# Moving a one-column constant so that the streamed matmul operands start 32 bytes earlier in SBUF

## The chip, the cores and the metric

One Trainium2 chip, one of its cores. The metric is the device time of one execution in microseconds (us). TensorE is PE in the profile (its weight loads are the row PEld), VectorE is DVE, ScalarE is ACT, GpSimd is POOL and SyncE is SP.

## The reference

A gated linear attention (4 batches, 8 heads, 768 steps, head size 48, a complex decay per channel) feeds a feed-forward block with a leaky ReLU. Cut to what matters here:

```python
for t in range(S):                      # per batch and head
    S_re, S_im = a_re_n * S_re - a_im_n * S_im + k v^T, a_re_n * S_im + a_im_n * S_re
    y[t] = q[t] @ S_re
x = y.reshape(3072, 384)                # tokens by channels
h = x @ w_in                            # 384 -> 2048
out = np.maximum(0.01 * h, h) @ w_out   # 2048 -> 384
```

## The kernel before, in words

The tokens are cut into 24 units of 128 (one chunk of one batch each). Attention is done in chunked form: `prep` (line 655) makes running decay products on DVE and ACT, `relay_of` (line 860) moves them to another partition layout by DMA, and `attend` (line 904) makes scores, masks them and forms the 128 output columns of its unit. Two units make one group `g` of `GT` = 256 tokens; there are 12 groups.

The feed-forward part works on one group at a time and splits every fp32 operand into a high part of type fp32r and a remainder, also fp32r. `attend` leaves the group's input as the tile `x` (high and low part, each 3 blocks of 256 columns). `first(g, s)` (line 1062) makes a block of `h`: for each of 2 blocks of 128 hidden channels and each of the 3 blocks of `x` it does three matmuls, high by high, high by low, low by high. `hide` (line 1074) applies the leaky ReLU on ACT and DVE and splits the result into the tile `hid`. `second(g, s)` (line 1089) streams `hid` against `wout_hi` and `wout_lo` into three banks of PSUM. So a group has 8 x 18 matmuls of `first` and 8 x 18 of `second`, 288 in all, and the kernel has 12 x 288 = 3,456 of them. In each, the weights (128 x 128 of `win_hi`, `win_lo`, `wout_hi` or `wout_lo`) are stationary and are loaded for that matmul, and 256 columns of `x` or `hid` are streamed: 1,024 contiguous bytes in each partition.

The four weight tiles are made at the start by `convert` (line 582) from 64-bit data. Its PE part (lines 641 to 643) has three matmuls per slab of 384 columns: two in fp32 against `ident`, and one in fp32r that streams a slab of `win_hi` or `wout_hi` against the stationary `nid`.

The order on each engine is set at build time: `drive` (line 236) runs all tasks against planned costs, and `Lane` (line 102) chains each engine's instructions in the planned order. The planner's costs are functions of shapes and kinds of instructions; they do not look at addresses. All compute instructions go through one call in `Lane`, so nearly all rows of the profile carry its line, 111.

Where things lie in a partition follows from the order of the pools and the sizes of the tiles; each tile begins at a multiple of 32 bytes. The pool `keep` comes first (`acc`, `xacc`, `low`, `zfl`, `wacc`, `bad`: 96, 96, 32, 288, 96 and 32 bytes), then the pool `cp`:

```python
win_hi, win_lo, wout_hi, wout_lo   # 24,576 bytes each
ident, mask, pst, rst              # 512, 2,048, 96 and 7,168 bytes
lnc                                # 4 bytes, so 32 of its own
nid                                # 512 bytes
```

and then the pool `pp` with everything that is worked on: two buffers of `asb` (2,048 bytes each), `qkt` (12,384), `t96` (16,512), two of `x` (6,144), `v` (6,656), two of `a` (9,216), `kn` and the output staging (3,072 each), a staging tile (6,144), three of `hid` (4,096), then `sq`, `u1`, `qk`, `xs`, `tg` and small ones. From `x` to `hid` all these sizes are multiples of 512 bytes.

`lnc` holds the logarithm of 0.999. It is written once by DVE (line 498) and read by ACT as the bias of one `Exp` per attention stage (line 689). `low` holds four sums that ACT writes in the last stage (lines 853 and 855) and that DVE reads in the final check (line 279).

Of the kernel before, what the change touches and what calls it, by code (L numbers as in the profile page):

```python
# [7 lines left out]
F32 = mybir.dt.float32  # L8
# [13 lines left out]
P = 128  # L22
# [406 lines left out]
def body(ctx, tc, keep, a_in, qk_in, v_in, w_in, out):  # L429
    nc = tc.nc  # L430

    cp = ctx.enter_context(tc.tile_pool(name="cp", bufs=1))
# [13 lines left out]
    nsub = len(SUBS)  # L446
    acc = keep.tile([P, 2, nsub], F32, tag="acc", name="acc")
    xacc = keep.tile([P, NT // C], F32, tag="xacc", name="xacc")
    low = keep.tile([P, 4], F32, tag="low", name="low")
    zfl = keep.tile([P, nsub, 2 * TI], F32, tag="zfl", name="zfl")  # L450
    lnc = cp.tile([P, 1], F32, tag="lnc", name="lnc")
    wacc = keep.tile([P, 2, WCP * -(-NWC // WCK)], F32, tag="wacc", name="wacc")

    pe, dve, act = Lane(tc, nc.tensor, pe_cost), Lane(tc, nc.vector, dve_cost), Lane(tc, nc.scalar, act_cost)
# [813 lines left out]
```

## Time and profile before

| | |
|---|---|
| median of 3 runs | 635.88 us (634.34 to 636.84) |
| the profiled execution | 636.34 us |
| its span, first to last instruction | 634.6 us |
| mean granted TensorE clock | 0.979 |
| PE busy | 593.1 us, 93% of the span |
| DVE busy | 531.2 us, 84% |
| ACT busy | 378.6 us, 60% |

The busy time of an engine is the union of its instructions' times, so a PE that is busy all the time need not be at its peak: the matmuls are pipelined, and a row's mean duration is the latency of one matmul, which is longer than the distance from one start to the next (called the pitch below). The pitch is read from the starts in a timeline, or from a piece of the chain of waits that counts its instructions. [...]

### The profile page before, as it was taken

To read this page: it belongs to the slowest core of one execution; us is meant where nothing else is said; L and a number is where in the kernel's file an instruction comes from. 1 tells how busy PE (TensorE), PEld (TensorE's weight loads), DVE (VectorE), ACT (ScalarE), POOL (GpSimd) and SP (SyncE) were. 2 spreads that over 40 slices of the span, in tenths; PEclk is the share of its full clock that TensorE was granted. 3 is DMA by queue.
4 is the path that set the end of the run, shared out by engine and by line. 5 is a ranking of instruction groups with operands and counts; after the bars stand their busy time and mean duration, and the time that the engine had idled before them with its cause. 6 is when DMAs were issued, how large, how long until landed. Compare 5 with 4: busy or idle time off the path is not lost.

```text
span 634.6 us, 18137 instructions
## 1 busy us (share of the span) xinstructions
PE 593.1 (93%) x7714; PEld 554.4 (87%) x7714; DVE 531.2 (84%) x916; ACT 378.6 (60%) x838; POOL 10.2 (2%) x33
## 2 busy tenths in 40 slices
PE   4992999999989989999999999999999999999994
PEld 2451668899889979999999999999999999999994
DVE  6999999899898988999989989999999898644340
ACT  6975776465475474574764664664755734868641
POOL 2000100100000000000000000000000000000000
PEclk9996999999999989999999999999999999999998
DMA  8843721422424223233235044043142235667500
GB/s 347 323 133 121 250 80 52 152 80 60 142 82 119 83 76 102 106 98 106 81 108 173 3 131 150 14 150 120 56 125 104 89 108 186 185 207 269 194 1 30
DMA packets 30200, 79.25 MB, mean 125 GB/s; under 512 B 5120, under 2 KB 11264, under 8 KB 30112
## 3 DMA queue, kind: packets, MB, share of 16 engines
q1 hardware_dynamic: 29728, 77.23, 37.5%
q8 instruction: 62, 1.02, 0.6%
q0 software_dynamic: 384, 0.79, 0.5%
q14 instruction: 26, 0.21, 0.1%
HBM read 54.26 MB, written 4.72 MB: 93 GB/s over the span
## 4 chain that ended last, share of the span: by engine, by line
PE 64%; DVE 23%; DMA 5%; ACT 4%; issue 2%; SPq 0%; DVEq 0%; ACTq 0%
PE ph L111 26%; PE po L111 26%; PE att L111 11%; DMA a<-in_a_dram 4%; DVE qkt L111 4%; DVE a L111 4%; DVE u L111 3%; DVE hid L111 2%; PE pd L111 2%; DVE sq L111 2%; DVE tg L111 1%; DVE xs L111 1%; DVE asb L111 1%; ACT sq L111 1%; DVE wcv L111 1%
## 5 line engine op out<-in xcount | busy, mean ns | idle before, releaser
L111 PE MATMUL po<-hid,wout_hi 128*128 128x256 f32 x1152 | 224.8, 284 | 0.0
L111 PE MATMUL ph<-x,win_hi 128*128 128x256 f32 x1152 | 217.3, 287 | 5.5 <-ACT x L111 3.3
L111 PEld LDWEIGHTS ph<-x,win_hi 128*128 128x128 f32 x1152 | 180.7, 191 | 7.9 <-ACT x L111 3.5
L111 PEld LDWEIGHTS po<-hid,wout_hi 128*128 128x128 f32 x1152 | 184.3, 189 | 1.2 <-issue 0.6
L111 PE MATMUL ph<-x,win_lo 128*128 128x256 f32 x576 | 164.1, 285 | 0.0
L111 PE MATMUL po<-hid,wout_lo 128*128 128x256 f32 x576 | 143.2, 284 | 0.0
L111 PEld LDWEIGHTS ph<-x,win_lo 128*128 128x128 f32 x576 | 109.7, 190 | 0.0
L111 PEld LDWEIGHTS po<-hid,wout_lo 128*128 128x128 f32 x576 | 109.2, 190 | 0.0
L111 ACT ACTIVATE tg<-ph 128x512 f32<-128x512 f32 x96 | 57.0, 594 | 74.2 <-PE ph L111 74.2
L111 DVE TENSOR_TENSOR tg<-ph,tg 128x512 f32<-128x512 f32 x96 | 65.7, 686 | 35.7 <-ACT tg L111 35.5
L111 ACT CAST hid<-tg 128x512 fp32r<-128x512 f32 x96 | 59.1, 616 | 47.5 <-DVE tg L111 47.3
L111 DVE TENSOR_TENSOR hid<-tg,hid 128x512 fp32r<-128x512 f32 x96 | 65.7, 686 | 14.3 <-ACT hid L111 13.4
L111 DVE TENSOR_TENSOR u<-a 128x384 f32<-128x384 f32 x84 | 46.5, 554 | 2.9 <-ACT a L111 1.4
L111 DVE TENSOR_TENSOR qkt<-qk,a 128x768 f32<-128x768 f32 x48 | 45.1, 952 | 3.9 <-ACT qkt L111 3.7
L111 PE MATMUL att<-t 96*32 96x96 f32 (+3 forms) x1536 | 38.0, 251 | 2.5 <-DMA t<-qkt 0.9
L111 PEld LDWEIGHTS att<-t 96*32 96x32 f32 x1536 | 33.7, 144 | 6.7 <-issue 1.5
L111 PE MATMUL att<-asb,v 128*32 128x128 f32 x768 | 37.1, 275 | 0.1
L111 ACT ACTIVATE rst<-rst,t 96x48 f32<-96x48 f32 x128 | 30.6, 322 | 8.3 <-DVE rst L111 8.3
L111 ACT COPY kn<-att 128x384 f32<-128x384 f32 x40 | 18.9, 476 | 27.5 <-PE att L111 23.0
L111 PE MATMUL att<-t,rst 96*32 96x128 f32 x640 | 32.3, 272 | 0.0
L111 DVE TENSOR_TENSOR asb<-att,mask 128x512 f32<-128x512 f32 x48 | 31.0, 683 | 1.1 <-PE att L111 0.9
L111 DVE TENSOR_TENSOR a<-u 128x192 f32<-128x192 f32 x84 | 29.8, 354 | 1.8
(171 smaller groups left out, 777.8 us busy)
## 6 DMA issues: line engine op xcount, KB each, us to landing
t<-qkt SPq DMA_DIRECT2D x92, 145.1 KB, 3.0
wck<-in_w_dram SPq DMA_DIRECT2D x10, 1152.0 KB, 6.1
v<-in_v_dram SPq DMA_DIRECT2D x12, 832.0 KB, 4.4
a<-in_a_dram SPq DMA_DIRECT2D x12, 768.0 KB, 4.7
qk<-in_qk_dram SPq DMA_DIRECT2D x12, 768.0 KB, 5.9
out_dram<-ot SPq DMA_DIRECT2D x12, 384.0 KB, 2.7
t<-qkt SPq DMA_DIRECT2D x46, 64.5 KB, 2.5
stage_st<-in_w_dram SPq DMA_DIRECT2D x3, 768.0 KB, 9.2
```

What stands on the lines that cost most here:

```text
L111: x = getattr(self.engine, name)(*args, **kw)
```

## The change

The tile `lnc` in the pool `cp` goes away. `low`, in the pool `keep`, gets a fifth column, and `lnc` becomes a view of that column.

```diff
-    low = keep.tile([P, 4], F32, tag="low", name="low")
+    low = keep.tile([P, 5], F32, tag="low", name="low")
     zfl = keep.tile([P, nsub, 2 * TI], F32, tag="zfl", name="zfl")
-    lnc = cp.tile([P, 1], F32, tag="lnc", name="lnc")
+    lnc = low[:, 4:5]
```

With 20 bytes instead of 16, `low` still fills one block of 32 bytes. `cp` is 32 bytes shorter, so `nid` and every tile of `pp` begin 32 bytes earlier. `x` and `hid` began at a multiple of 512 bytes plus 96 and now begin at a multiple of 512 plus 64. The four weight tiles, `ident`, `mask`, `pst` and `rst` lie ahead of `lnc` and stay where they were. No instruction is added, removed or reordered by the text of the change.

## Rows read from the trace of the kernel before

**Rows 1.** The page: busy time and instructions of each engine.

```profile
PE 593.1 (93%) x7714; PEld 554.4 (87%) x7714; DVE 531.2 (84%) x916; ACT 378.6 (60%) x838; POOL 10.2 (2%) x33
```

**Rows 2.** The chain that ended last: its shares by line.

```profile
by line: PE ph L111 25.7%; PE po L111 25.6%; PE att L111 11.3%; DMA a<-in_a_dram 4.5%; DVE qkt L111 4.3%; DVE a L111 4.1%; DVE u L111 3.4%; issue 2.2%; DVE hid L111 1.7%; PE pd L111 1.7%; DVE sq L111 1.6%; DVE tg L111 1.4%; DVE xs L111 1.1%
```

**Rows 3.** Busy time by stretch: us, PE, PEld, DVE, ACT, POOL, PEclk, DMA, GB/s.

```profile
20.00:40.00 20.00, 18.34 (x57) 9.98 (x56) 19.79 (x38) 16.50 (x30) 0.16 (x1) 1.00 0.70 255
...
344.69:389.38 44.69, 44.69 (x658) 43.87 (x657) 41.13 (x70) 26.43 (x64) 0.12 (x1) 1.00 0.32 98
389.38:434.07 44.69, 44.69 (x659) 43.89 (x657) 41.13 (x70) 26.42 (x64) 0.12 (x1) 1.00 0.32 103
...
500.00:600.00 100.00, 100.00 (x1229) 97.75 (x1221) 64.44 (x104) 62.45 (x124) 0.12 (x1) 1.00 0.60 193
```

**Rows 4.** Groups by line: the feed-forward matmuls (busy, mean ns of one).

```profile
L111 PE MATMUL po<-hid,wout_hi 128*128 128x256 f32 x1152 | 224.8, 284 | 0.0
L111 PE MATMUL ph<-x,win_hi 128*128 128x256 f32 x1152 | 217.3, 287 | 5.5 <-ACT x L111 3.3 <-DVE x L111 1.3 <-DVE tg L111 0.9
...
L111 PE MATMUL ph<-x,win_lo 128*128 128x256 f32 x576 | 164.1, 285 | 0.0
L111 PE MATMUL po<-hid,wout_lo 128*128 128x256 f32 x576 | 143.2, 284 | 0.0
```

**Rows 5.** The chain in order of time, 326 to 336 us (start, us, what).

```profile
326.99 4.32 PE po L111 x36
331.31 4.32 PE ph L111 x36
```

**Rows 6.** Timeline near 30.6 us: the weight conversion on PE and PEld.

```profile
30.61 0.19 PEld L111 LDWEIGHTS pd<-wout_hi,nid 128*128 128x128 f32 x1 [1.43 <-ACT wout_hi L111]
30.61 0.44 PE L111 MATMUL pd<-wout_hi,nid 128*128 128x384 f32 x1 [0.79 <-ACT wout_hi L111]
30.72 0.36 PEld L111 LDWEIGHTS pd<-stage_v,ident 128*128 128x128 f32 x2
...
30.89 0.50 PE L111 MATMUL pd<-stage_v,ident 128*128 128x384 f32 x1
```

**Rows 7.** Timeline near 607 us: feed-forward matmuls and their weight loads (start, us).

```profile
606.99 0.28 PE L111 MATMUL po<-hid,wout_lo 128*128 128x256 f32 x1
606.99 0.19 PEld L111 LDWEIGHTS po<-hid,wout_hi 128*128 128x128 f32 x1
607.11 0.28 PE L111 MATMUL po<-hid,wout_hi 128*128 128x256 f32 x1
607.11 0.19 PEld L111 LDWEIGHTS po<-hid,wout_lo 128*128 128x128 f32 x1
...
607.23 0.29 PE L111 MATMUL po<-hid,wout_lo 128*128 128x256 f32 x1
607.23 0.19 PEld L111 LDWEIGHTS po<-hid,wout_hi 128*128 128x128 f32 x1
```

**Rows 8.** The tiles lnc and low: durations (min/median/max), first and last start.

```profile
L111 ACT ACTIVATE u<-u,lnc x12: 926/936/941, 9.0 to 492.7; 128x768 f32<-128x768 f32 x12
L111 DVE MEMSET lnc<- x1: 59/59/59, 2.0 to 2.0; 128x1 f32 x1
...
L111 DVE TENSOR_SCALAR scr<-low x4: 142/142/143, 611.5 to 611.7; 128x1 f32<-128x1 f32 x4
```

**Rows 9.** Timeline of PE near 308 us: attention's output matmuls.

```profile
307.80 0.41 PE L111 MATMUL att<-t,rst 96*32 96x128 f32 x8
308.02 0.40 PE L111 MATMUL att<-asb,v 128*32 128x128 f32 x8
308.24 0.40 PE L111 MATMUL att<-t,rst 96*32 96x128 f32 x8
308.46 0.40 PE L111 MATMUL att<-asb,v 128*32 128x128 f32 x8
```

**Rows 10.** Groups by line: DVE instructions of the same shape on different tiles.

```profile
L111 DVE SCALAR_TENSOR_TENSOR qkt<-qkt 128x768 f32<-128x768 f32 x12 | 11.4, 949 | 0.0
L111 DVE TENSOR_TENSOR sq<-sq 128x768 f32<-128x768 f32 x12 | 11.4, 949 | 0.0
```

**Rows 11.** The chain in order of time: the pieces of the first loads.

```profile
0.82 4.50 DMA a<-in_a_dram
...
65.57 6.46 DMA a<-in_a_dram
```

## Prediction

> **What bounds the kernel now.** I read the busy times first: PE is at work for 593.1 of 634.6 us [rows 1]. That alone says little of a pipelined engine, so the chain of waits comes next: the feed-forward matmuls of `first` and `second` hold 25.7% and 25.6% of it, attention's matmuls 11.3%, and DVE's lines lie between [rows 2]. Then the stretches: a group takes 44.69 us in the middle, in which PE never pauses and DVE works for 41.13 us; after 500 us DVE is at 64% and PE still at 100% [rows 3]. So over most of the span the pitch of the matmuls sets the time, with DVE close behind it. Their durations of 284 to 287 ns [rows 4] are latencies. The pitch stands in the chain: 36 matmuls in 4.32 us, twice in a row, for `hid` and for `x` alike, which is 120 ns each [rows 5]. All 3,456 together are 3,456 x 0.120 = 414.7 us, and the chain's 51.3% are 325.6 us, so 79% of them lie on the path that sets the end.
>
> **What 120 ns are made of** decides the case, since x and hid are the operands that the change moves. [...] In the weight conversion a matmul of the same type streams 384 columns of `wout_hi`; its weights and those of the next matmul are issued 0.11 us apart, and the next matmul begins 0.28 us after it [rows 6]. Taking the first load off, the stream lasted 0.28 - 0.11 = 0.17 us. [...]
>
> This is the row that I lean on. The sizes in the text of the kernel put `wout_hi` at a multiple of 512 bytes plus 256: `x` is at plus 96, `asb`, `qkt` and `t96` ahead of it put the start of `pp` at plus 384, and the 108,672 bytes of `cp` ahead of that put its start, and each weight tile, at plus 256. [...]
>
> [...] Each feed-forward matmul begins together with the load of the next weights, and the next such pair comes 0.12 us later [rows 7]; two loads that nothing holds up come 0.11 us apart [rows 6]. A load that may start only when the matmul before it has taken its weights gives a loop of 0.11 us and a handover of some 10 ns, which is 120 ns whatever the stream needs, as long as the stream ends within it. The weight tiles don't move. In the conversion the load (0.11) is shorter than the stream (0.17), so there the stream decides.
>
> **The change, part by part.** Taken away: one tile; the write to `lnc` stays (59 ns, once, at 2.0 us), and the 12 activations that read it stay (936 ns) [rows 8]. Cost: 0. Reading the bias from `low` might add an order between those reads, the last at 492.7 us, and the writes to `low` after it; both are ACT's, in that order already, and DVE reads `low` at 611.5 us only [rows 8]. Cost: 0, and no one waits newly. No queue gets another order, SP's and POOL's included, since the planner's costs don't see addresses.
>
> Moved by 32 bytes: `nid` and all of `pp`. For attention's matmuls `asb` goes from a multiple of 128 (plus 384) to plus 352. The rows hold both kinds side by side: eight with `asb` as the stream and eight with `t96`, whose slices begin at steps of 516 bytes, take 0.22 us each, turn by turn [rows 9]. Cost: 0; with a rounding step of 0.01 us in each turn the bound is 5% of attention's 11.3%, or 3.6 us either way. For DVE the intermediate halves of `qkt` begin 3,096 bytes into their tile, which is no multiple of 16, and take 949 ns like `sq` [rows 10]. Cost: 0. For the loads by DMA no row shows one size at two offsets; the pieces of the chain that hold them are 4.50 us at the start and 6.46 us at 65.57 us [rows 11]. I take 0; a tenth of these two, 1.1 us either way, is the bound.
>
> Moved by 32 bytes too, and the question itself: `x` and `hid`. I take 0, by the loop above. [...]
>
> [...]
>
> The sum is 0. The profiled execution took 636.34 us, 1.7 beyond its span and 0.5 above the median, so I forecast **636.0**, the median. What a measurement of this kernel can tell from no change is about 0.5%, 3.2 us.
>
> **Rivals.**
>
> *A, the stream is the bound and its start costs.* [...] Against: the loop of loads gives 120 without it. [...]
>
> *B, the moved stream meets the weight load.* Both read SBUF in the same 120 ns; the weights stay at plus 256 and the stream shifts against them. Place: each feed-forward matmul. [...] For: nothing between 96 and 64 is measured, so a worse place is as open as a better one. [...]
>
> *C, nothing moves*, because the constant's block had stood elsewhere than the text implies. Then the time stays, as in the forecast, and I count it there.
>
> **How the numbers follow.** No change, the loop of loads or C, gets 0.49: two independent rows speak for it, but both rest on starts rounded to 0.01 us. A gets 0.36, as the kernel spends half its chain in exactly the operands that move, and B 0.15. The likeliest case alone would lie between 632 and 640, by attention's 3.6 us either way with the loads' 1.1 largely inside. The range takes in B's 646 and, on A's side, its 627 and half of the way on to 613, to 618; beyond these I leave out about 0.15. Faster by over 0.5% is A, slower B.
>
> **What would show it.** [...] The group's 44.69 us follows by 288 pitches, and if it shrinks, DVE's share of it must rise above 41.13 of 44.69. Eight attention matmuls should keep 0.22 us, `sq` and `qkt` 949 ns, `lnc`'s activation 936. The forecast is wrong if the pitch differs from 120 ns by more than 1.1 ns (3.2 us on the 79%), whatever the reason; it is wrong in its reason if the pitch stays and the time still moves, for then one of the parts costed at 0 has a price.

## The result, and the profile after

The changed kernel takes **630.43 us** (median of 10 runs, 628.78 to 633.21) against 636.52 for the kernel before (10 runs, 634.34 to 640.63): a ratio of 0.9900, 95% interval 0.9876 to 0.9924. That is 6.1 us or 1.0% faster. The forecast was no change; the time lies inside the range given, but on rival A's side.

The page of the changed kernel, busy time and instructions by engine, which answers to [rows 1]:

```profile
PE 586.4 (93%) x7714; PEld 546.8 (87%) x7714; DVE 530.3 (84%) x916; ACT 378.0 (60%) x838; POOL 10.1 (2%) x33
```

PE has the same number of instructions and 6.7 us less work, its weight loads 7.6; no other row changes by as much as 1 us. The span is 629.3 us, 5.3 less than before. Next the chain of waits of the changed kernel, its shares by line, its first load (against [rows 11]) and the two pieces that answer to [rows 5] (start, us, what):

```profile
by line: PE po L111 26.0%; PE ph L111 24.6%; PE att L111 15.6%; DVE a L111 4.3%; DVE qkt L111 3.9%; DVE u L111 3.1%; DMA a<-in_a_dram 2.6%; issue 2.4%; DVE hid L111 1.8%; DVE sq L111 1.6%; PE pd L111 1.4%; DVE tg L111 1.4%; DVE asb L111 1.3
...
0.82 4.57 DMA a<-in_a_dram
...
326.16 4.24 PE po L111 x36
330.40 4.24 PE ph L111 x36
```

36 matmuls take 4.24 us where they took 4.32: 117.8 ns for each instead of 120. Here is the change, and it is the same for `hid` and for `x`. The table by stretch (us, PE, PEld, DVE, ACT, POOL, PEclk, DMA, GB/s) says the same of a group; its rows answer to those of the middle in [rows 3]:

```profile
326.50:370.55 44.05, 44.05 (x659) 43.24 (x658) 41.04 (x70) 26.57 (x65) 0.12 (x1) 1.00 0.33 102
370.55:414.60 44.05, 44.05 (x658) 43.24 (x657) 41.04 (x70) 26.50 (x65) 0.12 (x1) 1.00 0.33 102
```

44.05 instead of 44.69 us: 0.64 less, and 288 pitches shorter by 2.2 ns are 0.63. The granted clock is 1.00 in these stretches of both kernels, so the clock is not the cause. DVE's 41.04 us stay below the group's time.

What the prediction had costed at nothing stayed where it was, as far as rows show it. First attention's output matmuls of the changed kernel in PE's timeline (against [rows 9]: eight in 0.22 us, turn by turn), then the tile `low`, which now holds the constant (against [rows 8]; duration min/median/max in ns), then the two DVE groups of [rows 10]:

```profile
307.17 0.40 PE L111 MATMUL att<-t,rst 96*32 96x128 f32 x8
307.39 0.40 PE L111 MATMUL att<-asb,v 128*32 128x128 f32 x8
307.61 0.40 PE L111 MATMUL att<-t,rst 96*32 96x128 f32 x8
307.83 0.40 PE L111 MATMUL att<-asb,v 128*32 128x128 f32 x8
```

```profile
L111 ACT ACTIVATE u<-u,low x12: 926/937/940, 9.0 to 489.6; 128x768 f32<-128x768 f32 x12
...
L111 DVE MEMSET low<- x1: 59/59/59, 2.0 to 2.0; 128x1 f32 x1
```

```profile
L111 DVE TENSOR_TENSOR sq<-sq 128x768 f32<-128x768 f32 x12 | 11.4, 950 | 0.0
L111 DVE SCALAR_TENSOR_TENSOR qkt<-qkt 128x768 f32<-128x768 f32 x12 | 11.4, 949 | 0.0
```

In the chain, attention's share rose from 11.3% to 15.6% and that of the loads of `a` fell from 4.5% to 2.6%. The matmuls above are as long as before, and the first load takes 4.57 us where [rows 11] has 4.50; the shares say by which waits the path ran in one execution, not how long a thing takes. No row isolates the price of the moved loads.

**Where in the span the time was saved.** ACT copies each group's result out of PSUM when its last matmul is done; these copies date the groups. From ACT's timeline of the kernel before, groups 0, 3, 4 and 11 (start, us, instruction, idle time before it):

```profile
139.58 0.93 ACT L111 COPY ot<-po 128x256 f32<-128x256 f32 x3
...
286.41 0.92 ACT L111 COPY ot<-po 128x256 f32<-128x256 f32 x3 [1.30 <-PE po L111]
...
331.11 0.92 ACT L111 COPY ot<-po 128x256 f32<-128x256 f32 x3 [1.56 <-PE po L111]
...
626.27 0.92 ACT L111 COPY ot<-po 128x256 f32<-128x256 f32 x3 [4.21 <-PE po L111]
```

The same four of the changed kernel:

```profile
141.66 0.93 ACT L111 COPY ot<-po 128x256 f32<-128x256 f32 x3
...
286.13 0.92 ACT L111 COPY ot<-po 128x256 f32<-128x256 f32 x3 [1.09 <-PE po L111]
...
330.21 0.93 ACT L111 COPY ot<-po 128x256 f32<-128x256 f32 x3 [1.41 <-PE po L111]
...
621.13 0.92 ACT L111 COPY ot<-po 128x256 f32<-128x256 f32 x3 [4.09 <-PE po L111]
```

After the first group the changed kernel is 2.1 us late, at the fourth it is 0.3 us ahead, and at the end 5.1. So of the 5.3 us in the span nearly all come from the eight groups behind 286 us, some 0.6 us each. Ahead of 286 us PE pauses. In the trace of the kernel before, PE is busy for 36.83 of the 50 us from 50 to 100, 44.33 of the 47 from 140 to 187 and 48.69 of the 52 from 187 to 239. DVE works for 47.31, 44.73 and 45.08 us of these, the chain ahead of 286 us holds loads of `a` of 5.34 to 6.75 us, and the granted clock falls to 0.86 in the first and 0.90 in the last. The clock between 50 and 100 us was 0.86 in the profiled execution before and 0.80 in that of the changed kernel, which goes with the late first group; one kernel profiled twice, below, shows a difference of this kind without any change of the layout.

### The profile page after: what moved, and what is told of

It is laid out like the page before. It is cut to its first block, busy times and chain, and to the rows that moved or that the text cites. A ratio compares the mean times of both kernels' runs of the same rounds, so it can differ in the third digit from the quotient of the medians.

```text
span 629.3 us, 18137 instructions
## 1 busy us (share of the span) xinstructions
PE 586.4 (93%) x7714; PEld 546.8 (87%) x7714; DVE 530.3 (84%) x916; ACT 378.0 (60%) x838; POOL 10.1 (2%) x33
## 4 chain that ended last, share of the span: by engine, by line
PE 68%; DVE 22%; ACT 4%; DMA 3%; issue 2%; DVEq 0%; ACTq 0%
PE po L111 26%; PE ph L111 25%; PE att L111 16%; DVE a L111 4%; DVE qkt L111 4%; DVE u L111 3%; DMA a<-in_a_dram 3%; DVE hid L111 2%; DVE sq L111 2%; PE pd L111 1%; DVE tg L111 1%; DVE asb L111 1%; ACT qkt L111 1%; DVE stage_st L111 1%; ACT sq L111 1%
## 5 line engine op out<-in xcount | busy, mean ns | idle before, releaser
L111 PE MATMUL po<-hid,wout_hi 128*128 128x256 f32 x1152 | 220.2, 282 | 0.0
L111 PE MATMUL ph<-x,win_hi 128*128 128x256 f32 x1152 | 210.6, 282 | 3.5 <-DVE x L111 1.2
L111 PEld LDWEIGHTS po<-hid,wout_hi 128*128 128x128 f32 x1152 | 182.0, 188 | 1.2 <-issue 0.6
L111 PEld LDWEIGHTS ph<-x,win_hi 128*128 128x128 f32 x1152 | 175.9, 187 | 6.1 <-DVE x L111 1.6
L111 PE MATMUL ph<-x,win_lo 128*128 128x256 f32 x576 | 160.7, 279 | 0.0
L111 PE MATMUL po<-hid,wout_lo 128*128 128x256 f32 x576 | 140.0, 279 | 0.0
L111 PEld LDWEIGHTS ph<-x,win_lo 128*128 128x128 f32 x576 | 108.2, 188 | 0.0
L111 PE MATMUL att<-t 96*32 96x128 f32 (+3 forms) x1536 | 37.8, 251 | 3.3 <-DMA t<-qkt 2.3
L111 ACT ACTIVATE rst<-rst,t 96x48 f32<-96x48 f32 x128 | 30.6, 323 | 8.7 <-DVE rst L111 8.7
L111 ACT ACTIVATE wck<-wck 128x1152 f32<-128x1152 f32 (+1 forms) x22 | 27.5, 1250 | 6.4 <-DMA wck<-in_w_dram 6.3
```

The lines of the kernel that those rows point to most:

```text
L111: x = getattr(self.engine, name)(*args, **kw)
```

## The experiments

Two things changed at once: the place of the constant and the start of all streamed tiles. And the start itself can matter in two ways: by itself (rival A's mechanism), or by its **distance** to the weights that are loaded while the stream runs (rival B's, with the sign open). In all that follows the distance is the stream's start less the weights' start, modulo 512 bytes. The weight tiles begin at 256, so the kernel before has (96 - 256) modulo 512 = 352 and the changed one 320. Slices of weights and of streams begin at multiples of 512 bytes within their tiles, so all matmuls of a kernel have one distance unless the text says otherwise.

The edits are made to the changed kernel. A `gap` is an unused tile that takes room and moves what lies behind it. Pitches are means over all back-to-back feed-forward matmuls, from their starts in the trace; by that reading the kernel before has 119.96 ns and the changed one 117.58.

### The constant alone

```diff
     lnc = low[:, 4:5]
+    cp.tile([P, 8], F32, tag="gap", name="gap")
```

> The constant stays in low, but 32 unused bytes take its old place, so x and hid are back at a multiple of 512 plus 96. Theory 1 (where the stream begins) and theory 2 (how far the stream lies from the weights, which stay at plus 256): the pitch goes back to 120.0 ns, 36 matmuls in 4.32 us, and the time to 636 us, 1.0% over the changed kernel. Theory 3 (the constant itself, its new neighbours or its new place): the pitch stays at 117.8 ns, 36 in 4.24 us, and the time at 630.

Measured: 636.35 us against 636.97 (medians of 10 and 13 runs), ratio 0.9992, interval 0.9963 to 1.0021. The chain's pieces of this kernel:

```profile
326.96 4.32 PE po L111 x36
331.28 4.32 PE ph L111 x36
```

The constant lies in `low` and the streams at plus 96: pitch and time are those of before. The constant's move is worth nothing that these runs can show; the 32 bytes are worth the change.

### Weights and streams moved together

```diff
+    keep.tile([P, 8], F32, tag="gap", name="gap")
```

The gap stands in the pool ahead of the weights: weights at plus 288, streams at plus 96, distance 320.

> 32 unused bytes ahead of the weight tiles: weights at plus 288, x and hid at plus 96, so each lies 32 bytes later than in the changed kernel and their distance is the same. Theory 1 (the stream's own start decides, plus 64 good, plus 96 bad): pitch 120.0 ns, about 636 us. Theory 2 (the distance decides): 117.8 ns, about 630 us.

One run: 631.07 us, pitch 117.6 ns. Its chain:

```profile
325.99 4.24 PE po L111 x36
330.23 4.24 PE ph L111 x36
```

This is the run that decides between the mechanisms. The streams begin at plus 96, as in the kernel before, and have the changed kernel's pitch; what else differs is that the weights moved with them. What counts is the distance, not the stream's own start.

### Only x moved

```diff
     for x in STAGES:
+        if x[0] == "v":
+            pp.tile([P, 8], F32, tag="gap", name="gap")
         add_stage(*x)
```

> 32 unused bytes between x and the tiles behind it: x at plus 64, hid at plus 96, weights at plus 256. By theories 1 and 2 alike the matmuls that stream x keep 117.8 ns (36 in 4.24 us) and those that stream hid go back to 120.0 (4.32 us), and the time lies half way, 633 us. If one operand sets both, by a rhythm that is kept from one matmul to the next, both show one pitch.

One run: 634.86 us, 1.9 over the half way that was expected; pitch of `first` 117.56 ns, of `second` 119.85. Its chain shows the two side by side:

```profile
328.00 4.32 PE po L111 x36
332.32 4.24 PE ph L111 x36
```

In this run the pitch of each half of a group follows its own stream: 117.56 ns where it is at plus 64, 119.85 where it is at plus 96.

### Four distances: 0, 256, 288 and 384

```diff
     nid = cp.tile([P, P], F32R, tag="nid", name="nid")
+    cp.tile([P, 48], F32, tag="gap", name="gap")
```

> 192 unused bytes behind the weights and nid: x and hid at plus 256, as the weights. Theory 1, in the form that a multiple of 64 is enough: 117.8 ns and 630 us. Theory 2: a pitch of its own, since the distance modulo 512 is now 0; if the two reads meet most there, 120 ns or more and 636 us or more. My prediction's reading (the load of the weights sets the loop) gave 120.0 at every start and has already failed at plus 64.

The streams begin at plus 256 like the weights. One run: 636.91 us, pitch 119.9. The chain of it:

```profile
327.66 4.32 PE po L111 x36
331.98 4.32 PE ph L111 x36
```

A stream that begins at a multiple of 256 bytes is as slow as one at plus 96. Alignment as such buys nothing here.

```diff
+    cp.tile([P, 112], F32, tag="gap", name="gap")
```

> x and hid at a multiple of 512, weights at plus 256: distance (start of the stream less start of the weights, modulo 512) 256, where the kernel before has 352, the changed one 320 and the stream at plus 256 had 0. If only a narrow stretch of distances near 320 is good: 120.0 ns and 636 us. If the cost falls steadily with the distance from 352 downwards: below 117.8 ns and 630 us. If only a distance of 0 and odd multiples of 32 are bad: 117.8 ns.

Streams at a multiple of 512, distance 256. One run: 638.33 us, pitch 119.9, the pitch of distance 0.

```diff
-    pst = cp.tile([P, 2, TI, B], F32, tag="pst", name="pst")
+    pst = keep.tile([P, 2, TI, B], F32, tag="pst", name="pst")
...
+    cp.tile([P, 16], F32, tag="gap", name="gap")
```

> The tile pst (96 bytes) moved ahead of the weights and 64 unused bytes behind nid: weights at plus 352, stream at plus 128, distance 288, one step of 32 below the changed kernel's 320. Narrow stretch around 320: 120.0 ns, 636 us, or one more good step. Steady fall: under 117.8 ns, under 630 us. Odd multiples of 32 bad: 120.0 ns.

Weights at plus 352, streams at plus 128. One run: 628.28 us, pitch 116.7, better than the change.

```diff
+    cp.tile([P, 16], F32, tag="gap", name="gap")
```

> 64 unused bytes behind nid: stream at plus 128, weights at plus 256, distance 384, one step of 32 above the kernel before. Narrow stretch around 320 or steady fall: 120.0 ns or more, 636 us or more. Only 0 and odd multiples of 32 bad: 117.8 ns and 630 us.

Streams at plus 128 again, weights back at 256. One run: 639.5 us, pitch 119.2. The time is above the kernel before's though the pitch isn't: by the output copies its third group ended at 246.6 us, against 241.7 before, so the loss lies ahead of that. With the kernel of distance 288 it makes a second pair with one stream start and two pitches.

### The other half of the circle: 192, 160, 224 and 448

```diff
+    cp.tile([P, 96], F32, tag="gap", name="gap")
```

> 384 unused bytes behind nid: stream at plus 448, weights at plus 256, distance 192. Narrow stretch: 120.0 ns, 636 us. Steady fall: the lowest pitch so far, at 113 ns some 621 us. Only 0 and odd multiples of 32 bad: 117.8 ns, 630 us.

One run: 623.43 us, pitch 114.6, 13 us under the kernel before. The chain:

```profile
324.53 4.08 PE po L111 x36
328.61 4.08 PE ph L111 x36
```

```diff
+    cp.tile([P, 88], F32, tag="gap", name="gap")
```

> 352 unused bytes behind nid: stream at plus 416, weights at plus 256, distance 160. So far the pitch was 120.0 ns at distances 0, 256 and 352, 119.2 at 384, 117.6 at 320, 116.7 at 288 and 114.6 at 192. If the cost repeats every 256 bytes with its best stretch between 160 and 224: 113 to 115 ns and 621 to 624 us. If it falls from 256 to 192 and on: 113 or less. If it climbs again towards 128 as it does at 384: 117 to 119 ns, 629 to 634 us.

One run: 629.99 us, pitch 117.8.

```diff
+    cp.tile([P, 104], F32, tag="gap", name="gap")
```

> 416 unused bytes behind nid: stream at plus 480, weights at plus 256, distance 224. Best stretch between 160 and 224: 113 to 115 ns, 621 to 624 us. If the cost of 256 (120.0 ns) begins here already: 117 to 120 ns, 630 to 636 us.

One run: 637.52 us, pitch 118.3. Here time and pitch part: by its pitch this kernel should lie under the one before. Its feed-forward part does, with 44.2 us per group between 291 and 512 us (the table below). The loss lies ahead of it. Each chain holds a load of `a` near 203 us; first the chain of the changed kernel, then of this one:

```profile
202.95 6.45 DMA a<-in_a_dram
```

```profile
204.22 8.23 DMA a<-in_a_dram
```

1.8 us are that load, and another 1.3 us had come before it. By the copies this kernel ends its third group at 246.9 us and the changed one at 242.0, so 4.9 of the 6.5 us between the spans (635.8 and 629.3) had come by then. Why the load took longer wasn't tried.

```diff
+    cp.tile([P, 32], F32, tag="gap", name="gap")
```

> 128 unused bytes behind nid: stream at plus 192, weights at plus 256, distance 448, which is 192 and another 256. If the cost repeats every 256 bytes (0 and 256 gave the same 120.0 ns): 114.6 ns as at 192, 623 us. If the period is 512: a pitch of its own, near the 119 to 120 ns of 384 and 0, and 634 to 637 us.

One run: 620.88 us, pitch 114.2. Distances 192 and 448 agree to 0.4 ns, as 0 and 256 do: at these pairs the pattern repeats after 256 bytes.

### High and low weights at two distances

```diff
     win_hi = cp.tile([P, TI, DFF], F32R, tag="win_hi", name="win_hi")
+    cp.tile([P, 88], F32, tag="gap0", name="gap0")
...
     nid = cp.tile([P, P], F32R, tag="nid", name="nid")
+    cp.tile([P, 8], F32, tag="gap", name="gap")
```

Distance 192 to `win_hi`, 352 to the other three. `first` uses `win_hi`, `win_hi`, `win_lo` in turn, so it can tell whether a stream meets its own weights or the next ones, which are loaded while it runs.

> 352 unused bytes behind win_hi and 32 behind nid: the stream (plus 448) has distance 192 to win_hi (plus 256) and 352 to win_lo, wout_hi and wout_lo (plus 96). In first the matmuls come as high, high, low weights. If the load of the next weights is what the stream meets: the step from the second high to the low one is long (the low weights are loaded under it), the step from low to high short. If a matmul's own weights decide: the step from low to the next high is long, the one to low short. In second all distances are 352, so 120.0 ns in both. The mean of first lies between 113 and 120, the time near 633 us.

One run: 633.3 us; pitch of `first` 118.0, of `second` 119.8. PE's timeline of it (start, us of the merged row, instruction):

```profile
330.23 0.40 PE L111 MATMUL ph<-x,win_hi 128*128 128x256 f32 x2
330.46 0.28 PE L111 MATMUL ph<-x,win_lo 128*128 128x256 f32 x1
330.58 0.40 PE L111 MATMUL ph<-x,win_hi 128*128 128x256 f32 x2
...
331.99 0.40 PE L111 MATMUL ph<-x,win_hi 128*128 128x256 f32 x2
```

The rounding hides the single steps: five rounds of three in 1.76 us, 0.352 us each. From the unrounded starts of all such steps in the trace: 114.5 ns from the first high matmul to the second, while `win_hi` is loaded; 122.8 from the second to the low one, while `win_lo` is loaded; 116.1 from the low one back, while `win_hi` is loaded. In the kernel before the three are 121.0, 119.0 and 119.8. The long step is the one whose *next* weights lie at distance 352. The low matmul itself, whose own weights lie there, is short. Unequal steps alone say little: in `second` of this run all distances are 352, and there too the step from high to low takes 122.3 ns and the one back 117.6 (119.2 and 120.7 in the kernel before). What counts is that in `first` the three steps spread over 8.3 ns, where the kernel before has 2.0, and that the long one is the one expected if the load under the stream counts. In this run the step follows the distance to the load that runs under it.

### The best distance, timed

The kernel with a gap of 32 words (128 bytes) once more, over five runs.

> The kernel of distance 448 again, over rounds: if the pitch of 114.2 ns holds from run to run, 621 us and a ratio of 0.975 to the kernel before. If the shorter rhythm of 113.3 ns was caught by chance, up to 630 us and a spread over several us.

Measured: **622.8 us** (5 runs, 622.31 to 626.03) against 636.85, ratio 0.979, interval 0.9766 to 0.9814. It beats the kernel before by 2.1% and the changed one by 7.6 us. Its chain, and a group of it in the table by stretch:

```profile
326.45 4.08 PE po L111 x36
330.53 4.08 PE ph L111 x36
```

```profile
326.45:369.40 42.95, 42.95 (x659) 42.17 (x658) 40.76 (x70) 26.87 (x64) 0.12 (x1) 1.00 0.34 106
```

The group is down to 42.95 us with 40.76 of DVE's work in it; PE still never pauses. Since this kernel was profiled twice, it also shows what executions differ by. The stretch from 50 to 100 us, first in the earlier profile, then in this one:

```profile
50.00:100.00 50.00, 36.64 (x425) 26.34 (x426) 47.84 (x87) 32.07 (x74) 2.74 (x6) 0.86 0.40 132
```

```profile
50.00:100.00 50.00, 36.27 (x395) 25.06 (x395) 44.77 (x81) 31.01 (x73) 2.74 (x6) 0.80 0.41 135
```

The same kernel, the same layout: a granted clock of 0.86 and 0.80, the first output copy at 139.25 and 143.76 us, spans of 619.1 and 622.5.

### Steps of 16 bytes, and 64

```diff
-    win_hi = cp.tile([P, TI, DFF], F32R, tag="win_hi", name="win_hi")
...
+    wide = cp.tile([P, 4 * TI * DFF + 8], F32R, tag="wide", name="wide")
+    win_hi, win_lo, wout_hi, wout_lo = (
+        wide[:, 4 + i * TI * DFF : 4 + (i + 1) * TI * DFF].rearrange("p (k f) -> p k f", k=TI if i < 2 else NFC)
+        for i in range(4)
+    )
...
+    cp.tile([P, 24], F32, tag="gap", name="gap")
```

The weights are views that begin 16 bytes into one tile: weights at plus 272, streams at plus 192.

> The four weight tiles as views into one tile, 16 bytes into it, and 96 unused bytes behind nid: weights at plus 272, stream at plus 192, distance 432. If the cost is a smooth function of the distance: between 114.2 ns (448) and the pitch of 416 (by the period, 117.8 of 160): 115 to 117 ns, 624 to 628 us. If it goes in steps of 32: 114.2 or 117.8.

One run: 635.77 us, pitch 118.7.

```diff
+    cp.tile([P, 32], F32, tag="gap", name="gap")
```

With the same `wide`: streams at plus 224, distance 464.

> The same with 128 unused bytes: stream at plus 224, distance 464. Smooth: between 114.2 ns (448) and 118.3 (224, by the period 480): 115 to 117 ns, 624 to 629 us. Steps of 32: 114.2 or 118.3. A best place beyond 448: 113.3 ns throughout, 618 us.

One run: 632.83 us, pitch 118.0. Sixteen bytes to either side of 448 lose most of what it gains; both pitches lie outside the 115 to 117 ns that a smooth course would have given. In both kernels the weights also start at an odd multiple of 16 bytes; no run keeps that at a distance of 448, so which of the two costs isn't shown.

```diff
+    cp.tile([P, 64], F32, tag="gap", name="gap")
```

> 256 unused bytes behind nid: stream at plus 320, distance 64, which is 256 below the changed kernel's 320. Period of 256: 117.6 ns and 630 us. Period of 512: another pitch.

Without `wide`, streams at plus 320. One run: 632.5 us, pitch 117.7, the pitch of distance 320: the third pair that is 256 bytes apart and agrees.

### All of them together

The group is a fifth of the time between the output copies of groups 3 and 8, from each trace; it leaves the early stretch out, in which executions differ. The last column is the group worked out from the pitch: 44.68 less 288 x (119.96 - pitch).

| distance | kernel | pitch, ns | time, us | group, us | from the pitch |
|---|---|---|---|---|---|
| 0 | stream at 256 | 119.9 | 636.91 | 44.66 | 44.66 |
| 64 | gap of 256 bytes | 117.7 | 632.5 | 44.08 | 44.03 |
| 160 | gap of 352 | 117.8 | 629.99 | 43.96 | 44.06 |
| 192 | gap of 384 | 114.6 | 623.43 | 43.00 | 43.14 |
| 224 | gap of 416 | 118.3 | 637.52 | 44.24 | 44.20 |
| 256 | gap of 448 | 119.9 | 638.33 | 44.66 | 44.66 |
| 288 | weights and streams moved | 116.7 | 628.28 | 43.76 | 43.74 |
| 320 | the changed kernel | 117.6 | 630.43 (median) | 44.08 | 44.00 |
| 352 | the kernel before | 119.96 | 636.52 (median) | 44.68 | 44.68 |
| 384 | gap of 64 | 119.2 | 639.5 | 44.58 | 44.46 |
| 432 | weights 16 bytes in | 118.7 | 635.77 | 44.34 | 44.32 |
| 448 | gap of 128, timed | 114.2 | 622.8 (median) | 42.94 | 43.02 |
| 464 | weights 16 bytes in | 118.0 | 632.83 | 44.18 | 44.12 |

The group follows the pitch to 0.14 us in every row. The time of one run follows it less well, since the first 240 us add several us of their own.

## Why the prediction was wrong

**What bounds the kernel** was read rightly: the pitch sets the time where PE never pauses, and there the gain is 288 pitches per group. The share was about right as well: 2.38 ns x 3,456 = 8.2 us, times 79% = 6.5, against 6.1 measured. Only the 79% do not lie evenly: in the two traces 4.9 of the 5.3 us come from the groups behind 286 us and 0.3 from the first four.

**The parts costed at nothing** cost nothing: the constant (ratio 0.9992 with its interval around 1), attention's 0.22 us, DVE's 949 and 950 ns, the activation's 937. For the loads by DMA only the first one, 4.50 and 4.57 us, can be set side by side.

**The step that failed** is the row that the prediction leaned on, the conversion's: 0.17 us for 384 columns from plus 256 stood beside 120 ns for 256 columns from plus 96, and the start was taken to be harmless. How much of either the columns alone need isn't shown. What the pitch of the feed-forward matmuls follows is the distance to the weights that are loaded under the stream, 114.2 to 119.96 ns in the table, and the conversion's row can't show that. Two things were wrong with it as a control. Its 0.17 us came from starts rounded to 0.01 us: from the unrounded starts the step from the load of `ident` to the next matmul is 172.0 ns (mean of 28 such pairs at a granted clock of 1.00). And it did not react to the distance where runs changed it. The load under the stream there is that of `ident` [rows 6], which begins right behind the four weight tiles, so also at plus 256: distance 0, where the table has 119.9 ns. But in the run with high and low weights apart `win_hi` lies at distance 160 from `ident`, and its pairs take 172.2 ns; with the weights 16 bytes in the distance is 496, and they take 172.4 and 170.2. Why the conversion's stream doesn't feel what the feed-forward's does is open. A start at plus 256 in the feed-forward part itself had the full 119.9 ns, and with the same loads the pitch went to 114.2, 5.8 ns down.

**The loop of loads** fell too: "120 ns whatever the stream needs". That a load waits until the matmul before it has taken its weights was the author's estimate; no row shows it. The loads were left as they are in the kernel with a gap of 128 bytes, and 36 matmuls took 4.08 us. The 0.11 us between loads [rows 6] may still be a floor below that; no kernel here held a pitch under 113.3 ns.

**The rivals.** A's 627 and B's 646 both come from a price of 3.3 ns per matmul, and the 613 behind A's end of the range from 10 ns; no run shows either. In their place the runs showed 2.4 ns less for the change and, over all the distances, a pitch of 114.2 ns at the lowest. So A had the size nearly right (measured were 630.4 us) without a measured ground, and the mechanism wrong: with weights and streams moved by 32 bytes the start was plus 96 again and the pitch stayed at 117.6. B had the mechanism right as far as the pitch follows the place of the stream relative to the weights that are loaded under it, and the sign wrong: it priced the move as a loss, where the kernel before, with 119.96 ns, already stood at one of the slowest distances that were tried.

**Two small sums** of the prediction were off and decided nothing: half of the way from 627 to 613 is 620, not 618, and 3.2 us on 79% of the matmuls are 1.2 ns, not 1.1.

**What stays open.** Why distances of 192 and 448 are the best of those tried, and the neighbours of 448 16 bytes away are not: the runs give the pattern, not what in SBUF makes it. And why one kernel holds two rhythms. In PE's timeline of the changed kernel, a round of three matmuls near 94 us, then one near 330 us:

```profile
94.00 0.39 PE L111 MATMUL ph<-x,win_hi 128*128 128x256 f32 x2
94.22 0.28 PE L111 MATMUL ph<-x,win_lo 128*128 128x256 f32 x1
94.33 0.39 PE L111 MATMUL ph<-x,win_hi 128*128 128x256 f32 x2
...
330.60 0.40 PE L111 MATMUL ph<-x,win_hi 128*128 128x256 f32 x2
330.83 0.28 PE L111 MATMUL ph<-x,win_lo 128*128 128x256 f32 x1
330.95 0.40 PE L111 MATMUL ph<-x,win_hi 128*128 128x256 f32 x2
```

0.33 us near 94 us, 0.35 near 330: from the unrounded starts 113.3 and 117.8 ns per matmul, at one distance and with a granted clock of 1.00 in both stretches. In this trace a rhythm holds through each unbroken run of feed-forward matmuls, and changes only where PE paused or attention's matmuls came between.

This bears on the best distances too. By the unrounded starts the kernels of distances 64, 192 and 448 hold the same two rhythms, 113.3 and 117.8 ns. Behind 290 us the fast one has none of the steps at 64 and 320, about three quarters at 192, and about nine tenths in both profiles of 448. So the 114.2 to 114.6 ns of 192 and 448 are means of two rhythms, and between these four distances what changes is how often each is taken. What makes TensorE take one or the other is open: in the first profile of 448 one change, at 138.3 us, came without a pause, where `first` followed `second`. Whether a kernel can be made to hold the fast one at distance 320 wasn't tried.

## What to carry to other kernels

Where each matmul's weights are loaded under the stream of the one before, the place of the streamed tile relative to the weights can be a parameter of its own: in this kernel the constant's move and 128 unused bytes together took 2.1% off, and the 32 bytes of an unrelated tile alone had cost 1.0%. Read the pitch from pieces of the chain that count their instructions, before and after any change of the layout, also of one that isn't meant for speed. And a row taken as a control must be known to react to the thing that is in question: the conversion's step stays at 170 to 172 ns at distances of 0, 160 and 496, so it said nothing of what sets the feed-forward's pitch.

## What the runs showed of the hardware that was not expected

- The pitch of these matmuls follows the distance in a partition between the stream and the weights that are loaded under it: 114.2 to 120.0 ns for 256 columns, with a pattern that agreed at the three pairs tried 256 bytes apart (119.9 and 119.9 at 0 and 256, 117.7 and 117.6 at 64 and 320, 114.6 and 114.2 at 192 and 448). Sixteen bytes either way from 448, with the weights at an odd multiple of 16, the pitch was 118.7 and 118.0, about 4 ns more.
- At distances 64, 192, 320 and 448 one kernel holds two rhythms, 113.3 ns and 117.8; in the changed kernel the granted clock was 1.00 in the stretches of both.
- The granted clock of an early stretch, 50 to 100 us, was 0.80 or 0.86 in two executions of one kernel, and the first group ended 4.5 us apart. Single runs of a kernel whose start is bound by other engines should be compared by a later stretch.
